# A fused attention and gMLP block on one core: head sums in pairs, and another order of loads and bias at the front

## The chip, the core and the metric

The kernel runs on one core of a Trainium2 chip. The metric is the device time of one execution in microseconds (us); the median of three runs is 208.47 us, from 208.3 to 208.62. A profile of one execution goes with it. Names of engines: PE is TensorE (PEld its weight loads), DVE is VectorE, ACT is ScalarE, POOL is GpSimd, SP is SyncE, which only issues DMAs here. An engine with a q behind its name is that engine's queue of DMA issues.

## The reference

x has 2048 tokens of 512 features, bf16. It is normalized once (xn), and two branches and x itself are summed:

```python
xn = layernorm(x)
# A: 32 heads of 16; each token attends to 8 tokens, 2 apart, up to itself
q, k, v = split(xn @ wqkv)
logits[h, s, w] = sum_d q[h, s, d] * k[h, s - 2 * w, d] / 4     # -1e9 ahead of token 0
a = softmax(logits, axis=w) mixed with v[h, s - 2 * w, :] @ wo
# B: gated MLP with a mix over tokens; F = 1376, halves of 688
z1, z2 = split(gelu(xn @ w_in));  z2 = layernorm(z2)
b = (z1 * (w_sp @ z2 + b_sp[:, None])) @ w_out
out = x + a + b
```

## The kernel before

The 2048 tokens are 16 tiles of 128. The order of instructions on every engine is the order of the program text (a manual schedule): a statement's position decides where it stands in the queue of its engine, and nothing is moved by a planner. Waits come from data and from buffers that are used again.

*Front (lines 91 to 397).* SP issues the loads in the order of lines 166 to 178: tokens of tile 0, of tile 1, the first half of w_z2 (the z2 half of w_in, 2 of 4 k-chunks), tokens of tiles 2 and 3, the second half of w_z2, tokens 4 to 7, q and k weights, tokens 8 to 11, wv, the bias b16, tokens 12 to 15. The x buffers (xqp) are three, so the load of tokens 12 to 15 into the fourth group needs the first buffer back. spin(n) issues n matmuls of a tile of ones into a PSUM tile that nobody reads. DVE takes statistics (ln_stats, L185 and L186) and normalizes (ln_apply, L190). Tiles 0 to 3 are transposed by TensorE (transpose_pe, L212; copied out by ACT for tiles 0 and 1, by DVE for 2 and 3), tiles 4 to 15 by DMA transposes on SP's queue (transpose_dma, L219), in groups of two whose 1/sqrt is worked out by DVE and POOL (ln_newton). z2_part(i, pz, kc) issues the two z2 matmuls (344 columns each) of k-chunk kc of tile i; z2_start does all four chunks, z2_gelu evacuates with gelu, z2_square sums squares on ACT.

*Middle (lines 399 to 480).* q and k chunks (qk_pair L272, qk_chunk L260), z2 tiles, v matmuls (v_pair, L285) and attention logits follow one another on TensorE. For logits, DVE multiplies q with shifted k for two window positions at once, products(hb, p) for block hb of 1024 tokens and pair p (L301, two buffers pr), and TensorE sums over the 16 features of each head: reduce_heads(hb, p), 16 matmuls with a 0/1 selector of 32 columns, placed in the four column strips of the array (tile_position, L310), evacuated by ACT (L312). v_pair works in the same strips, 32 matmuls each. softmax_top subtracts the maximum (DVE), softmax_exp is on ACT, softmax_norm on DVE. z2_stats and z2_norm (L252, 16 DVE instructions) normalize z2.

*Late (lines 492 to 661).* mix(j) multiplies token tile j of w_sp with z2 (32 matmuls, L493) and adds the bias column b_col[:, j] on ACT (L496); z1_tile(j) computes the z1 half (L505, gelu L510); gate_out(j) multiplies on DVE (L515) and transposes by DMA. Between them DVE works off the attention mix (av_ops, L559 to L568). At the end TensorE multiplies with wo and w_out (L636, L647, L622) and DVE adds x.

PSUM: bank_pair gives two-bank tiles in turn from three, ps_aux two one-bank tiles for transposes, pb and head sums. The bias is a row vector of 16 x 128 that pb (L405) transposes into columns.

Of the kernel before, what the change touches and what calls it, by code (L numbers as in the profile page):

```python
# [7 lines left out]
BF16 = mybir.dt.bfloat16  # L8
# [5 lines left out]
P = 128  # L14
S = 2048
D = 512
NT = S // P
C = D // P
# [10 lines left out]
F = 1376  # L29
FH = 688  # L30
# [15 lines left out]
def kernel(  # L46
# [17 lines left out]
    A = nc.scalar  # L64
    G = nc.gpsimd
    PE = nc.tensor
    SP = nc.sync
# [17 lines left out]
    def bank_pair(name, two=False):  # L85
        turn[0] += 1
        pool = ps_b if turn[0] % 3 == 0 and not two else ps_a
        return pool.tile([P, 2, 512], F32, name=name, tag="mm")


    ones = const.tile([P, 256], BF16, name="ones")
    V.memset(ones[:], 1.0)
    idle = bank_pair("idle")

    def spin(n):
        for _ in range(n):
            PE.matmul(idle[:, 0, 0:256], ones[:, 0:P], ones[:], start=True, stop=True)

    spin(17)

    ident = const.tile([P, P], BF16, name="ident")
    G.memset(ident[:], 0.0)
# [11 lines left out]
    G.affine_select(out=mask[:], in_=mask[:], compare_op=ALU.is_ge, fill=NEG,  # L114
                    base=-DIL * (W - 1), pattern=[[DIL, W], [1, HALO]], channel_multiplier=0)
    b_col = const.tile([P, NT], F32, name="b_col")
    b16 = const.tile([NT, P], BF16, name="b16")
    stats = const.tile([P, NT, 6], F32, name="stats")
    mv = const.tile([P, NT, 2], F32, name="mv")
    rstd = const.tile([P, NT], F32, name="rstd")  # L120
# [37 lines left out]
    xq = []  # L158

    def load_x(b):  # L160
        t = xqp.tile([P, 4, D], BF16, name="xq")
        SP.dma_start(t[:], x2[b * 4 * P:(b + 1) * 4 * P, :].rearrange("(i p) d -> p i d", p=P))
        xq.append(t)

    x0 = xqp.tile([P, 4, D], BF16, name="xq")
    SP.dma_start(x0[:, 0, :], x2[0:P, :])
    SP.dma_start(x0[:, 1, :], x2[P:2 * P, :])
    SP.dma_start(w_z2[:, 0:2, :], w_in_r[:, 0:2, FH:F])
    SP.dma_start(x0[:, 2:4, :], x2[2 * P:4 * P, :].rearrange("(i p) d -> p i d", p=P))
    SP.dma_start(w_z2[:, 2:4, :], w_in_r[:, 2:4, FH:F])  # L170
    xq.append(x0)
    load_x(1)
    for s in range(2):
        SP.dma_start(wqk[:, :, s, :], wqkv_r[:, :, s * D:(s + 1) * D])
    load_x(2)
    SP.dma_start(wv[:], wqkv_r[:, :, 2 * D:3 * D])
    SP.dma_start(b16[:], B_b_sp.rearrange("(j p) -> j p", p=P))
    load_x(3)
    V.memset(qk[0][:, 1, :, 0:HALO], 0.0)
    V.memset(vp[0:32, :, 0, 0:HALO], 0.0)  # L180
# [2 lines left out]
    def ln_stats(i):  # L183
        xs = xq[i // 4][:, i % 4, :]
        V.bn_stats(stats[:, i, :], xs)  # L185
        V.bn_aggr(mv[:, i, :], stats[:, i, :])  # L186

    def ln_apply(i):
        xn = xnp.tile([P, D], BF16, name="xn")
        V.tensor_scalar(xn[:], xq[i // 4][:, i % 4, :], mv[:, i, 0:1], rstd[:, i:i + 1], ALU.subtract, ALU.mult)  # L190
        return xn

    def roots(a, b):
        A.activation(rstd[:, a:b], mv[:, a:b, 1], ACT.Sqrt, bias=eps_t[:])
# [14 lines left out]
    def transpose_pe(i, xn):  # L209
        pt = ps_aux.tile([P, C, P], BF16, name="pt", tag="aux")  # L210
        for c in range(C):
            PE.transpose(pt[:, c, :], xn[:, c * P:(c + 1) * P], ident[:])  # L212
        if i < 2:
            A.copy(xnT[:, :, i * P:(i + 1) * P], pt[:])
        else:
            V.tensor_copy(xnT[:, :, i * P:(i + 1) * P], pt[:])

    def transpose_dma(i, xn):
        SP.dma_start_transpose(xnT[:, :, i * P:(i + 1) * P], xn[:])  # L219

    def z2_start(i):
        pz = bank_pair("pzb")
        for kc in range(C):
            z2_part(i, pz, kc)
        return pz

    def z2_part(i, pz, kc):
        for hh in range(2):
            PE.matmul(pz[:, hh, 0:FHALF], xnT[:, kc, i * P:(i + 1) * P],  # L229
                      w_z2[:, kc, hh * FHALF:(hh + 1) * FHALF],  # L230
                      start=(kc == 0), stop=(kc == C - 1))
# [5 lines left out]
    def z2_square(i):  # L237
        A.activation(junk[:], z2[:, i, :], ACT.Square, accum_out=zsq[:, i:i + 1])  # L238

    def z2_tile(i):  # L240
        z2_gelu(i, z2_start(i))
# [13 lines left out]
    def qk_chunk(b, c):  # L255
        tsl = slice(b * 512, (b + 1) * 512)
        pq = bank_pair("pq")
        for s in range(2):
            for kc in range(C):
                PE.matmul(pq[:, s, :], wqk[:, kc, s, c * P:(c + 1) * P], xnT[:, kc, tsl],  # L260
                          start=(kc == 0), stop=(kc == C - 1))
        at = HALO + b % 2 * 512
        A.copy(qk[b // 2][:, :, c, at:at + 512], pq[:])  # L263
# [16 lines left out]
    def v_pair(d2):  # L280
        pv = bank_pair("pv")
        for dd in range(2):
            for kc in range(C):
                for k in range(NG):
                    PE.matmul(pv[32 * k:32 * k + 32, dd, :].rearrange("p (b t) -> p b t", b=NB),  # L285
                              wv_v[:, kc, 2 * d2 + dd, :], xnT_g[:, kc, :, k, :],
                              start=(kc == 0), stop=(kc == C - 1), tile_position=(0, 32 * k))
        A.copy(vp[:, 2 * d2:2 * d2 + 2, :, HALO:HALO + TG],
               pv[:].rearrange("p a (b t) -> p a b t", b=NB))
# [8 lines left out]
    def products(hb, p):  # L298
        pr = prp.tile([P, 2, C, SB], BF16, name="pr")
        off = HALO - DIL * (W - 1 - 2 * p)  # L300
        V.tensor_tensor(pr[:], qk[hb][:, 0, :, HALO:HALO + SB].unsqueeze(1).broadcast_to([P, 2, C, SB]),  # L301
                        shifted(qk[hb][:, 1, :, off:off + SB]), ALU.mult)
        prs[hb, p] = pr

    def reduce_heads(hb, p):
        pr = prs.pop((hb, p))
        pl = ps_aux.tile([P, 2, TG], F32, name="pl", tag="aux")
        for c in range(C):
            for k in range(NG):
                PE.matmul(pl[32 * k:32 * k + 32, :, :], rsel[:, c, :], pr[:, :, c, k * TG:(k + 1) * TG],  # L310
                          start=(c == 0), stop=(c == C - 1), tile_position=(0, 32 * k))
        A.activation(lg[hb][:, 2 * p:2 * p + 2, :], pl[:], ACT.Copy, scale=float(DH) ** -0.5)  # L312

    def softmax_top(hb):
        l = lg[hb]
        if hb == 0:
            V.tensor_tensor(l[0:32, :, 0:HALO], l[0:32, :, 0:HALO], mask[:], ALU.add)
        m4 = lgp.tile([P, 4, TG], BF16, name="m4", bufs=1)
        V.tensor_tensor(m4[:], l[:, 0:4, :], l[:, 4:8, :], ALU.max)
        V.tensor_tensor(m4[:, 0:2, :], m4[:, 0:2, :], m4[:, 2:4, :], ALU.max)  # L320
        V.tensor_tensor(m4[:, 0, :], m4[:, 0, :], m4[:, 1, :], ALU.max)
        V.tensor_tensor(l[:], l[:], m4[:, 0, :].unsqueeze(1).broadcast_to([P, W, TG]), ALU.subtract)
# [24 lines left out]
    def recip(i):  # L347
        V.reciprocal(rstd[:, i:i + 1], rstd[:, i:i + 1])

    ln_stats(0)  # L350
    roots(0, 1)
    ln_stats(1)
    roots(1, 2)
    recip(0)
    transpose_pe(0, ln_apply(0))
    recip(1)
    spin(2)
    transpose_pe(1, ln_apply(1))
    spin(2)
    pz0 = bank_pair("pzb")  # L360
    pz1 = bank_pair("pzb")
    for i, pz in ((0, pz0), (1, pz1)):
        for kc in range(2):
            z2_part(i, pz, kc)
    ln_stats(2)
    roots(2, 3)
    ln_stats(3)
    roots(3, 4)
    for kc in range(2, C):
        z2_part(0, pz0, kc)  # L370
    z2_gelu(0, pz0)
    recip(2)
    xn2 = ln_apply(2)
    recip(3)
    xn3 = ln_apply(3)
    transpose_pe(2, xn2)
    for kc in range(2, C):
        z2_part(1, pz1, kc)
# [8 lines left out]
    for g in groups + (None,):  # L387
        if g:
            for i in range(*g):
                ln_stats(i)  # L390
            ln_newton(*g)
        if prev:
            for i in range(*prev):
                transpose_dma(i, ln_apply(i))
        prev = g


# [3 lines left out]
    z2_square(1)  # L401
    qk_pair(0, 1, 0)
    qk_pair(0, 1, 1)
    pb = ps_aux.tile([P, NT], BF16, name="pb", tag="aux")
    PE.transpose(pb[:], b16[:], ident[0:NT, 0:NT])  # L405
    A.copy(b_col[:], pb[:])
    z2_tile(4)
    z2_square(2)
    z2_tile(5)
# [20 lines left out]
    qk_chunk(2, 1)  # L430
    z2_square(7)
    qk_chunk(2, 2)
    reduce_heads(0, 0)
    products(0, 2)
    v_pair(0)
    qk_chunk(2, 3)
    z2_tile(8)
    qk_chunk(3, 0)
    z2_square(8)
    qk_chunk(3, 1)  # L440
    reduce_heads(0, 1)
    products(0, 3)
    v_pair(1)
    qk_chunk(3, 2)
    z2_tile(9)
    qk_chunk(3, 3)
    z2_square(9)
    z2_tile(10)
    reduce_heads(0, 2)
    products(1, 0)  # L450
    v_pair(2)
    z2_square(10)
    z2_tile(11)
    z2_square(11)
    z2_tile(12)
    reduce_heads(0, 3)
    softmax_top(0)
    products(1, 1)
    v_pair(3)
    z2_square(12)  # L460
    z2_tile(13)
    z2_square(13)
# [1 line left out]
    z2_square(14)  # L464
    z2_tile(15)
    z2_square(15)


    v_pair(4)
    z2_stats()  # L470
    z2_norm()
    v_pair(5)
    reduce_heads(1, 0)
    products(1, 2)
    softmax_exp(0)
    v_pair(6)
# [36 lines left out]
    def gate_out(j):  # L513
        gs, z1 = gate.pop(j)
        V.tensor_tensor(z1[:, 0:FH], gs[:].rearrange("p a b -> p (a b)"), z1[:, 0:FH], ALU.mult)  # L515
        SP.dma_start_transpose(uT[:, :, j * P:(j + 1) * P], z1[:])

    g0 = mix(0)
    reduce_heads(1, 1)
    products(1, 3)  # L520
    z1_tile(0, g0)
    g1 = mix(1)
    reduce_heads(1, 2)
    softmax_norm(0, lgp)
    z1_tile(1, g1)
    gate_out(0)
    reduce_heads(1, 3)
    softmax_top(1)
    gate_out(1)
    z1_tile(2, mix(2))  # L530
    softmax_exp(1)
    att.close()

# [157 lines left out]
```

## Time and profile before

| | us |
|---|---|
| median of 3 runs | 208.47 |
| time of the profiled execution | 208.18 |
| span of its records | 206.5 |
| DVE, ACT, POOL busy | 166.2, 93.6, 16.1 |
| first spin on PE | 1.25 |
| first z2 matmul | 6.61 |
| first DMA transpose issued | 15.03 |
| mix(0) begins | 73.39 |
| last output tile added on DVE | 203.44 |

The span runs from the first to the last recorded instruction; 1.7 us of the execution's time lie around it. The profile gives for each engine its busy time, for each idle time what ended it, and the chain of work that ended last, followed back from the end. Matmuls are pipelined: a group's printed length holds the modelled end of its last matmul, so the distance from one start to the next tells more than a printed length. Starts of groups in the chain lie some 0.1 us behind those in the timeline for the same reason.

### The profile page before, as it was taken

The numbers are of one execution on the slowest core, as the hardware profiler recorded it, in microseconds if no ns is written. First come the engines' busy times: TensorE is split into PE (matmuls) and PEld (weight loads), VectorE is DVE, ScalarE is ACT, GpSimd is POOL, SyncE is SP. The second block draws the span as 40 slices with busy tenths as digits, with TensorE's granted clock in tenths as the row PEclk, the third lists the DMA queues.
The fourth block names the chain that finished last, engine by engine and source line by source line (L and its number), as shares of the span: only waits on it lengthen the run. The fifth ranks groups of instructions, "written<-read, shape, count | busy, mean of one in ns | idle before, by whom it ended". The sixth has DMA issues, their size and how long they took to land.

```text
span 206.5 us, 4016 instructions
## 1 busy us (share of the span) xinstructions
PE 201.7 (98%) x1644; PEld 118.3 (57%) x1644; DVE 166.2 (81%) x192; ACT 93.6 (45%) x145; POOL 16.1 (8%) x82
## 2 busy tenths in 40 slices
PE   7999999999999999999999999999999999999994
PEld 4754544545556665566666666666666664444442
DVE  4899939958369699999999999999999955582353
ACT  3777887675689996328633322123333311000000
POOL 5045630000000000000000000000000000000000
PEclk9999999999999999999999999999999999999999
DMA  6996546978000004623975999999544233036432
GB/s 166 318 344 101 103 101 146 236 136 157 3 0 3 3 0 43 134 51 76 174 156 123 231 179 195 217 190 187 122 141 120 45 79 42 25 97 209 115 104 90
DMA packets 67410, 25.63 MB, mean 124 GB/s; under 512 B 57168, under 2 KB 67264, under 8 KB 67264
## 3 DMA queue, kind: packets, MB, share of 16 engines
q1 hardware_dynamic: 67008, 25.24, 57.6%
q8 instruction: 13, 0.21, 0.4%
q10 hardware_dynamic: 384, 0.13, 0.3%
q14 instruction: 5, 0.04, 0.1%
HBM read 9.79 MB, written 2.10 MB: 58 GB/s over the span
## 4 chain that ended last, share of the span: by engine, by line
PE 91%; DVE 3%; DMA 3%; POOL 1%; issue 1%
PE pg L493 36%; PE pq L260 10%; PE po L647 10%; PE pz L505 9%; PE pzb L229 8%; PE pv L285 7%; PE po L636 6%; PE pl L310 4%; DMA xnT<-xn 2%; DVE stats L185 2%; DMA xq<-in_A_x_dram 1%; PE pt L212 1%; PE po L622 1%; DVE xn L190 1%; DVE mv L186 0%
## 5 line engine op out<-in xcount | busy, mean ns | idle before, releaser
L493 PE MATMUL pg<-z,wspT 128*128 128x344 bf16 x512 | 77.3, 309 | 0.0
L493 PEld LDWEIGHTS <-wspT 128*128 128x128 bf16 x512 | 49.9, 98 | 25.2 <-issue 0.8
L301 DVE TENSOR_TENSOR pr<-qk 128x8192 bf16<-128x8192 bf16 x8 | 35.1, 4425 | 6.5 <-PE pl L310 6.5
L496 ACT ACTIVATE gs<-pg,b_col 128x688 bf16<-128x688 f32 x16 | 13.3, 834 | 54.1 <-PE pg L493 54.1
L559 DVE TENSOR_TENSOR pw<-vp,a_sb 128x4096 bf16<-128x4096 bf16 x16 | 36.1, 2285 | 0.0
L651 DVE TENSOR_TENSOR ot<-po,xr 128x512 bf16<-128x512 f32 x15 | 10.2, 689 | 15.2 <-PE po L647 15.1
L260 PE MATMUL pq<-xnT,wqk 128*128 128x512 bf16 x96 | 21.7, 379 | 0.0
L505 PE MATMUL pz<-w_z,xnT 128*128 128x344 bf16 x128 | 21.3, 309 | 0.0
L229 PE MATMUL pzb<-w_z,xnT 128*128 128x344 bf16 x128 | 20.6, 309 | 0.3 <-DMA xnT<-xn 0.3
L647 PE MATMUL po<-wout,uT 128*128 128x512 bf16 x90 | 19.8, 379 | 0.0
L564 DVE TENSOR_TENSOR pw<-pw 128x4096 bf16<-128x4096 bf16 x8 | 18.3, 2288 | 0.1
L229 PEld LDWEIGHTS <-xnT 128*128 128x128 bf16 x128 | 12.0, 98 | 7.7 <-issue 0.8
L505 PEld LDWEIGHTS <-xnT 128*128 128x128 bf16 x128 | 12.4, 98 | 6.8 <-issue 0.8
L260 PEld LDWEIGHTS <-wqk 128*128 128x128 bf16 x96 | 9.2, 98 | 11.1 <-issue 0.8
L647 PEld LDWEIGHTS <-uT 128*128 128x128 bf16 x90 | 8.7, 98 | 11.0 <-issue 0.8
L285 PE MATMUL pv<-xnT,wv 128*32 128x512 bf16 x256 | 14.9, 380 | 0.0
L263 ACT CAST qk<-pq 128x1024 bf16<-128x1024 f32 x12 | 12.1, 1012 | 5.8 <-PE pq L260 5.8
L510 ACT ACTIVATE z<-pz 128x688 bf16<-128x688 f32 x16 | 11.9, 743 | 5.6 <-PE pz L505 4.8
L238 ACT ACTIVATE junk<-z 128x688 bf16<-128x688 bf16 x16 | 12.4, 778 | 0.1
L636 PE MATMUL po<-wo_r,op 32*128 32x512 bf16 x224 | 12.4, 374 | 0.0
L185 DVE BATCH_NORM_STATS2 stats<-xq 128x6 f32<-128x512 bf16 x16 | 10.8, 674 | 1.9 <-DMA xq<-in_A_x_dram 1.9
L234 ACT ACTIVATE z<-pzb 128x688 bf16<-128x688 f32 x16 | 11.8, 736 | 1.0 <-PE pzb L229 1.0
(79 smaller groups left out, 166.7 us busy)
## 6 DMA issues: line engine op xcount, KB each, us to landing
xr<-in_A_x_dram SPq DMA_DIRECT2D x4, 512.0 KB, 4.1
out_dram<-ot SPq DMA_DIRECT2D x15, 128.0 KB, 1.7
wo_r<-in_A_wo_dram SPq DMA_DIRECT2D x4, 448.0 KB, 5.0
xq<-in_A_x_dram SPq DMA_DIRECT2D x3, 512.0 KB, 8.4
wqk<-in_A_wqkv_dram SPq DMA_DIRECT2D x2, 512.0 KB, 7.5
w_z<-in_B_w_in_dram SPq DMA_DIRECT2D x2, 344.0 KB, 4.3
w_z<-in_B_w_in_dram SPq DMA_DIRECT2D x1, 688.0 KB, 7.2
wout<-in_B_w_out_dram SPq DMA_DIRECT2D x1, 640.0 KB, 4.7
```

The lines of the kernel that those rows point to most:

```text
L185: V.bn_stats(stats[:, i, :], xs)
L229: PE.matmul(pz[:, hh, 0:FHALF], xnT[:, kc, i * P:(i + 1) * P], w_z2[:, kc, hh * FHALF:(hh + 1) * FHALF], start=(kc == 0), stop=(kc == C - 1))
L260: PE.matmul(pq[:, s, :], wqk[:, kc, s, c * P:(c + 1) * P], xnT[:, kc, tsl], start=(kc == 0), stop=(kc == C - 1))
L285: PE.matmul(pv[32 * k:32 * k + 32, dd, :].rearrange("p (b t) -> p b t", b=NB), wv_v[:, kc, 2 * d2 + dd, :], xnT_g[:, kc, :, k, :], start=( ...
L301: V.tensor_tensor(pr[:], qk[hb][:, 0, :, HALO:HALO + SB].unsqueeze(1).broadcast_to([P, 2, C, SB]), shifted(qk[hb][:, 1, :, off:off + SB]), ...
L493: PE.matmul(pg[:, hh, 0:FHALF], wsps[j][:, k, :], z2[:, k, hh * FHALF:(hh + 1) * FHALF], start=(k == 0), stop=(k == NT - 1))
L496: A.activation(gs[:], pg[:, :, 0:FHALF], ACT.Identity, bias=b_col[:, j:j + 1])
L505: PE.matmul(pz[:, hh, 0:FHALF], xnT[:, kc, j * P:(j + 1) * P], w_z1[:, kc, hh * FHALF:(hh + 1) * FHALF], start=(kc == 0), stop=(kc == C - 1))
L559: V.tensor_tensor(pw[:], shifted(vp[:, :, hb, off:off + P]), a_sb[:, 2 * p:2 * p + 2, osl].unsqueeze(2).broadcast_to([P, 2, DH, P]), ALU.mult)
L564: V.tensor_tensor(pws[p - 1][:], pws[p - 1][:], pw[:], ALU.add)
L636: PE.matmul(pos[jj, k][:], op[32 * k:32 * k + 32, d, jj * P:(jj + 1) * P], wo_r[32 * k:32 * k + 32, d, :], start=(d == 0), stop=((jj, k, d ...
L647: PE.matmul(pos[jj, k][:], uT[:, m, i * P:(i + 1) * P], wout[:, m, :], start=False, stop=(m == MCH - 1))
```

## The change

Head sums. Before, each reduce_heads of block 0 stands ahead of one v_pair, and the later three of block 1 between mix and z1_tile calls. Now reduce_heads(0, 0) and (0, 1) stand together ahead of v_pair(0) and v_pair(1); (0, 2) and (0, 3) ahead of v_pair(2) and v_pair(3); (1, 0) and (1, 1) between v_pair(5) and v_pair(6); (1, 2) and (1, 3) between mix(2) and z1_tile(2). products and softmax calls move with them.

Front. w_z2 is loaded in one DMA behind tokens 0 to 3; z2_start(0) does all chunks of tile 0 before tile 1 begins. wv is loaded behind the DMA transposes of tiles 6 and 7. Tokens 12 to 15 are loaded into a part of a_sb, which is otherwise first written by softmax_exp(0). The bias is loaded by ACT's queue as the first statement, transposed between 26 and 9 spins and copied between the first two square roots. A spin has 128 columns in place of 256, and there are 26 + 9 + 4 + 4 of them in place of 17 + 2 + 2.

```diff
+    b16 = const.tile([NT, P], BF16, name="b16")
+    A.dma_start(b16[:], B_b_sp.rearrange("(j p) -> j p", p=P))
-    ones = const.tile([P, 256], BF16, name="ones")
+    ones = const.tile([P, P], BF16, name="ones")
...
-            PE.matmul(idle[:, 0, 0:256], ones[:, 0:P], ones[:], start=True, stop=True)
-    spin(17)
+            PE.matmul(idle[:, 0, 0:P], ones[:], ones[:], start=True, stop=True)
+    spin(26)
...
-        t = xqp.tile([P, 4, D], BF16, name="xq")
+        t = xqp.tile([P, 4, D], BF16, name="xq") if b < 3 else a_sb[:, 0:4, :]
...
     SP.dma_start(x0[:, 1, :], x2[P:2 * P, :])
-    SP.dma_start(w_z2[:, 0:2, :], w_in_r[:, 0:2, FH:F])
     SP.dma_start(x0[:, 2:4, :], x2[2 * P:4 * P, :].rearrange("(i p) d -> p i d", p=P))
-    SP.dma_start(w_z2[:, 2:4, :], w_in_r[:, 2:4, FH:F])
+    SP.dma_start(w_z2[:], w_in_r[:, :, FH:F])
...
     load_x(2)
-    SP.dma_start(wv[:], wqkv_r[:, :, 2 * D:3 * D])
-    SP.dma_start(b16[:], B_b_sp.rearrange("(j p) -> j p", p=P))
     load_x(3)
...
+    pb = ps_aux.tile([P, NT], BF16, name="pb", tag="aux")
+    PE.transpose(pb[:], b16[:], ident[0:NT, 0:NT])
+    spin(9)
     ln_stats(0)
     roots(0, 1)
+    A.copy(b_col[:], pb[:])
     ln_stats(1)
...
-    spin(2)
+    spin(4)
     transpose_pe(1, ln_apply(1))
-    spin(2)
-    pz0 = bank_pair("pzb")
-    pz1 = bank_pair("pzb")
-    for i, pz in ((0, pz0), (1, pz1)):
-        for kc in range(2):
-            z2_part(i, pz, kc)
+    spin(4)
...
-    for kc in range(2, C):
-        z2_part(0, pz0, kc)
+    pz0 = z2_start(0)
     z2_gelu(0, pz0)
...
+    pz1 = bank_pair("pzb")
+    for kc in range(2):
+        z2_part(1, pz1, kc)
     transpose_pe(2, xn2)
...
                 transpose_dma(i, ln_apply(i))
+            if prev[0] == 6:
+                SP.dma_start(wv[:], wqkv_r[:, :, 2 * D:3 * D])
...
-    pb = ps_aux.tile([P, NT], BF16, name="pb", tag="aux")
-    PE.transpose(pb[:], b16[:], ident[0:NT, 0:NT])
-    A.copy(b_col[:], pb[:])
...
     qk_chunk(2, 2)
-    reduce_heads(0, 0)
-    products(0, 2)
-    v_pair(0)
     qk_chunk(2, 3)
...
     qk_chunk(3, 1)
+    reduce_heads(0, 0)
     reduce_heads(0, 1)
+    products(0, 2)
     products(0, 3)
+    v_pair(0)
     v_pair(1)
...
     z2_tile(10)
+    z2_square(10)
+    z2_tile(11)
     reduce_heads(0, 2)
+    reduce_heads(0, 3)
     products(1, 0)
     v_pair(2)
-    z2_square(10)
-    z2_tile(11)
+    products(1, 1)
+    softmax_top(0)
     z2_square(11)
+    v_pair(3)
     z2_tile(12)
-    reduce_heads(0, 3)
-    softmax_top(0)
-    products(1, 1)
-    v_pair(3)
...
     reduce_heads(1, 0)
+    reduce_heads(1, 1)
     products(1, 2)
...
     g0 = mix(0)
-    reduce_heads(1, 1)
     products(1, 3)
     z1_tile(0, g0)
     g1 = mix(1)
-    reduce_heads(1, 2)
     softmax_norm(0, lgp)
     z1_tile(1, g1)
     gate_out(0)
+    g2 = mix(2)
+    reduce_heads(1, 2)
     reduce_heads(1, 3)
     softmax_top(1)
     gate_out(1)
-    z1_tile(2, mix(2))
+    z1_tile(2, g2)
```

More of the change, by code (lines that the diff above doesn't have):

```diff
@@ L116 @@
     b_col = const.tile([P, NT], F32, name="b_col")
-    b16 = const.tile([NT, P], BF16, name="b16")
     stats = const.tile([P, NT, 6], F32, name="stats")
@@ L160, in load_x @@
     def load_x(b):
-        t = xqp.tile([P, 4, D], BF16, name="xq")
-        SP.dma_start(t[:], x2[b * 4 * P:(b + 1) * 4 * P, :].rearrange("(i p) d -> p i d", p=P))
+        t = xqp.tile([P, 4, D], BF16, name="xq") if b < 3 else a_sb[:, 0:4, :]
+        SP.dma_start(t[:] if b < 3 else t, x2[b * 4 * P:(b + 1) * 4 * P, :].rearrange("(i p) d -> p i d", p=P))
         xq.append(t)
```

## The prediction

> **What bounds the kernel now.** I read the busy shares first, then the chain of work that ended last, then the timeline of TensorE over the first 23 us, then the DMA landings, then VectorE's timeline. The shares of the page:
>
> ```profile
> PE 201.7 (98%) x1644; PEld 118.3 (57%) x1644; DVE 166.2 (81%) x192; ACT 93.6 (45%) x145; POOL 16.1 (8%) x82
> ```
>
> TensorE is at work for all but a few us, and from 20.56 us to 203.4 us the chain consists of PE pieces alone. So there are only two ways to shorten the span: less time inside the PE pieces, or an earlier moment at which the gapless stretch begins. Pieces of the chain (start, length, what):
>
> ```profile
> 36.32 0.98 PE pl L310 x16
> 37.30 1.73 PE pv L285 x32
> 39.03 1.83 PE pq L260 x8
> ...
> 51.18 1.73 PE pq L260 x8
> ...
> 69.14 0.86 PE pl L310 x16
> ```
>
> Head sums (pl) and v matmuls (pv) use the array in column strips (128*32 in the page's groups), everything around them uses 128*128. A head sum entered from 128*128 work takes 0.98, one between v matmuls (69.14) takes 0.86: entering costs 0.12. The q/k chunk that follows strips takes 1.83, one that follows 128*128 work takes 1.73: leaving costs 0.10. Between pl and pv nothing is paid. **One strip stage costs 0.22 us of overhead.**
>
> TensorE at the front, twice (start, duration, instruction, in brackets the idle time and its releaser):
>
> ```profile
> 6.39 0.38 PE L97 MATMUL idle<-ones 128*128 128x256 bf16 x2
> 6.61 1.96 PE L229 MATMUL pzb<-w_z,xnT 128*128 128x344 bf16 x12
> 8.41 0.39 PE L212 MATMUL pt<-ident,xn 128*128 128x128 bf16 x4
> ```
>
> ```profile
> 18.46 0.38 PE L272 MATMUL pq<-xnT,wqk 128*128 128x512 bf16 x1
> 18.77 0.18 PE L405 MATMUL pb<-ident,b 16*128 16x16 bf16 x1
> 18.91 1.34 PE L229 MATMUL pzb<-w_z,xnT 128*128 128x344 bf16 x8
> 20.56 0.61 PE L229 MATMUL pzb<-w_z,xnT 128*128 128x344 bf16 x3 [0.31 <-DMA xnT<-xn]
> ```
>
> Twelve matmuls in 8.41 - 6.61 = 1.80 us is 0.15 each, so the ninth, the first that needs the second half of w_z2, starts at 7.81. That half was issued at 2.70 and took 5.1 us: it landed at 7.8, with no slack. DMA landings (KB, us from issue to landing; the 688 KB one is w_z1, later in the kernel):
>
> ```profile
> w_z<-in_B_w_in_dram SPq DMA_DIRECT2D x1, 344.0 KB, 5.1
> ```
>
> ```profile
> w_z<-in_B_w_in_dram SPq DMA_DIRECT2D x1, 688.0 KB, 7.2
> ...
> xq<-in_A_x_dram SPq DMA_DIRECT2D x2, 128.0 KB, 2.1
> ...
> uT<-op ACTq DMA_DIRECT2D x8, 16.0 KB, 3.9
> ...
> b<-in_B_b_sp_dram SPq DMA_DIRECT2D x1, 4.0 KB, 7.3
> ```
>
> **Part 1, head sums in pairs.** Strip stages before: (00 v0), (01 v1), (02 v2), (03 v3), (v4 v5 10 v6 v7), (11), (12), (13), eight, where 02 is the head sum of block 0, pair 2. In the order of instructions of the new kernel: (00 01 v0 v1), (02 03 v2 v3), (v4 v5 10 11 v6 v7), (12 13), four. Matmuls are the same in number. 4 x 0.22 = **-0.88 us** on the path.
>
> What the new order makes later is VectorE, since products have two buffers and a product waits for the head sum two before it. Laid out on the old clock, with the chain's lengths: q/k chunks to 42.67, head sum 00 to 43.65 instead of 37.3. The third product runs 43.75 to 48.2 (before, it followed at once: 13.09 for three from 31.15), the fourth to 52.6; head sum 03 starts at 56.0, so 3.4 us of slack. Head sum 02 ends at 56.0 (before 55.05), the products of block 1 run to 64.95, softmax_top (2.97, from 61.48 to 64.45 before) to 67.9. z2_stats started at 68.78 before, so it is not later. zrstd hangs on ScalarE's queue there (squares, v copy, table load at 69.55), which I lay out 0.2 earlier at most. mix(0) starts 0.86 later for head sum 11 and 0.44 earlier for two stages: 73.88.
>
> ```profile
> 71.47 6.00 DVE L252 TENSOR_SCALAR z<-z,zmean,zrstd 128x688 bf16<-128x688 bf16 x16
> ```
>
> The sixteenth tile is ready at 77.47, and mix(0) wants it at 73.46 + 15/16 x 4.67 = 77.84: 0.37 of cover before, about 0.8 after. If z2_norm came later than that, mix(0) would lose the difference one to one. softmax_top(1) now waits for head sum 13 (ends 92.17, plus 0.6 of evacuation): 92.9 instead of 92.18. VectorE runs about 0.8 late from there while TensorE is 0.9 early. This is covered:
>
> ```profile
> 171.01 0.52 DVE L515 TENSOR_TENSOR z<-gs,z 128x688 bf16<-128x688 bf16 x1 [2.90 <-ACT z L510]
> ```
>
> 2.90 idle here, 4.01 before 177.74, and op is done at 182.28 where TensorE asks for it at 186.77. Cost 0; without that cover 0.8.
>
> **Part 2, bias transposed at the beginning.** Out of the path go pb and its surroundings: the last q/k matmul before it is issued at 18.46 and lasts 0.216 (6.91/32), so z2_tile(4) could start at 18.68 instead of 18.91: **-0.23**. In its new place pb stands between 26 and 9 spins. Spins before: 17 of 256 columns, 1.25 to about 4.9, some 0.213 each; 35 of half that width are 3.73 us, with pb about 0.1 it ends near 5.1, before xn of token tile 0 (5.18). This needs the bias by 1.2 + 26 x 0.107 = 4.0. Behind SP's queue it took 7.3; alone on ACT's queue at 0.8 it stands nearest to the first 128 KB of x, 2.1 (2.9), the other ACT-queue row gives 3.9 (4.7). At 4.7 tile 0 starts 0.6 late, which the wait in part 3 hides; at 8.1 it would cost 1.7. I take 2.9, cost 0. Its issue and the table load (1.28) on ScalarE end before mv is there at 3.9; b_col's copy (0.18) fits between the two square roots (3.92+0.29 and 4.71). The removed copy on ScalarE at 19.79 is off the path.
>
> **Part 3, w_z2 in one load.** All of z2_start(0) now waits for all 688 KB. It is issued at 2.19, with the same 1200 KB ahead and in it as the second half had (landed 7.8, issued 2.70). Low end: the stretch from 4 to 5 us moved 331 GB/s, and next to nothing moved before 2 us, so 1200 KB could be over by 5.7 and told by about 6.1, before w_z2 is wanted (6.61): shift 0. High end: w_z1's 7.2 us as one load, 9.39: shift 2.8. I take the row with the same bytes at the same place, moved by the issue it saves (0.51): **7.3**, a shift of 0.7 with the start latency. Everything behind moves with it: transposes of tiles 2 and 3, VectorE's copies of them, statistics of tile 4 onward and the DMA transposes. **+0.7 us.** The 4 + 4 spins of 128 take what 2 + 2 of 256 took.
>
> The Trainium skill, "DMA: Bandwidth & Descriptors", section "Anatomy of one DMA — SWDGE (gpsimd) path", fits a load as 2.0 us plus bytes over 436 GB/s (on another queue type than SP's). By that, as an estimate, 688 KB land 3.6 us after issue at 5.8, nothing waits, and the sum would be 0.7 better; the trace's 5.1 and 7.2 speak against it.
>
> **Part 4, wv behind the transposes, x tiles 12 to 15 into a_sb.** 512 KB less lie ahead of the first DMA transposes, and the bias too. Tile 4's took 3.8 and tile 5's 4.1 (16.41 to 20.52) against a median of 2.5. z2_tile(5) could start at 18.91 + 1.17 = 20.08 and started at 20.56: **-0.48**. What is late next: with the shift s, tile 5 is issued at 16.4+s and lands 18.9+s, wanted 19.85+s; tile 7 issued 19.2+s lands 21.7+s, wanted 22.2+s. If landing stays near 3.5 to 4, 0.45 comes back; this end I keep for the range. wv itself is wanted at about 44 and lands near 25; SP's queue gets it before tile 8's transpose, whose group is wanted at 31 and then lands by 28. a_sb is written first by softmax_exp(0) at 73.9: no wait.
>
> **The sum.** -0.88 - 0.23 - 0.48 + 0.7 = -0.9 us. On the profiled execution, 208.18 (span 206.5), 207.3. The median of the runs shown, 208.47, lies 0.3 above it: **207.6** against the median. Less than 0.2%, 0.42 us, can't be told from no change.
>
> **Rivals.**
> - *The front eats the pairs* (0.22): w_z2 lands at 7.8 to 8.6, or strip stages do not cost what I read. Landing at 8.2 gives a shift of 1.6 and a sum of 0: 208.5. If pairs gave nothing, the front alone is -0.0: 208.5 as well. For it: the ninth matmul had no slack before and the first eight have now lost their early half. Against: issue is 0.5 earlier.
> - *w_z2 late, slower* (0.18): one load of 688 KB behaves as w_z1's did, 7.2, landing 9.39. Shift 2.8: sum +1.2, 209.7. It decides from a landing at 8.6 (+0.42). For it: the only whole load of this size in the trace. Against: w_z1 shared the engines with transposes of w_sp.
> - *Nothing waits* (part of the forecast's case): landing before 6.6, sum -1.6, 206.9.
>
> **Chances.** Forecast, landing from 6.6 to 7.8, -1.6 to -0.4: 0.60. Same 0.22, slower 0.18. Range 206.8 to 208.8: it holds the first two cases and the beginning of the third.
>
> Idle matmuls of 256 columns start 0.213 apart until about 6.2 us and 0.108 apart behind it, and TensorE then stays at the short distance. The Trainium skill, "TensorE: Matmul & The Clock Gate", section "What's actually happening", says that about 3.4 us without work bring the half rate back. By it a wait of 0.7 or of 2.8 costs only itself; were a wait enough to bring it back, the twelve first matmuls alone would take another 1.8. No row here shows it either way.
>
> **What would show it.** Right: pl pieces of 0.98 only at the head of four stages, each stage's follower 0.10 longer; a PE wait on w_z2 of about 0.7 near 6.6 us; no wait before z2_tile(5); no pb at 18.8; mix(0) gapless. Wrong: a DMA wait of over 1.5 us there, a VectorE releaser ahead of mix(0) or of the last PE stage, a late bias that holds the first transposes.

## The result and the profile after

The changed kernel takes 206.69 us (median of 4 runs, 206.6 to 206.94); the kernel before, beside it, 208.38 (4 runs, 208.25 to 208.62). The ratio is 0.992, interval 0.9902 to 0.9937: 1.7 us less, where 0.9 was predicted, and 0.1 below the low end of the range. The profiled execution took 206.6, its span 204.9, against 208.18 and 206.5: 1.6 us less, which the lines below account for.

The page of the changed kernel, its span and its busy shares:

```profile
span 204.9 us, 4056 instructions
...
PE 200.3 (98%) x1660; PEld 120.7 (59%) x1666; DVE 166.1 (81%) x192; ACT 93.5 (46%) x145; POOL 16.1 (8%) x82
```

TensorE is busy 1.4 us less, and its share is 98% as before: no idle time has come in the place of what went.

The chain of work that ended last, of the changed kernel (start, length, what): the strip stages, then mix(0).

```profile
42.11 1.84 PE pl L310 x32
43.95 3.45 PE pv L285 x64
...
50.41 1.73 PE pq L260 x8
...
54.47 1.84 PE pl L310 x32
56.31 3.45 PE pv L285 x64
...
68.15 1.73 PE pl L310 x32
69.87 3.45 PE pv L285 x64
73.33 4.77 PE pg L492 x32
...
89.77 1.84 PE pl L310 x32
91.61 1.27 PE pz L504 x8
```

Two head sums of 32 matmuls entered from other work take 1.84, that is 2 x 0.86 + 0.12; the pair that stands between v matmuls (68.15) takes 1.73. Leaving costs 0.10 (the z1 tile of 1.27 beside its usual 1.17). There are four stages instead of eight, each at the price that was read from before. From 12.38 to the last output add the chain holds PE pieces and five pieces of "issue" of 0.05 to 0.16 us, each beside a group whose records are one matmul short (47 of 48, 41 of 42 in the po groups). mix(0) begins without a wait.

TensorE at the front of the changed kernel (timeline: start, duration, instruction):

```profile
4.00 0.19 PE L351 MATMUL pb<-ident,b 16*128 16x16 bf16 x1
...
6.46 0.39 PE L100 MATMUL idle<-ones 128*128 128x128 bf16 x4
6.83 1.91 PE L229 MATMUL pzb<-w_z,xnT 128*128 128x344 bf16 x12
8.58 0.39 PE L212 MATMUL pt<-ident,xn 128*128 128x128 bf16 x4
...
18.85 3.66 PE L229 MATMUL pzb<-w_z,xnT 128*128 128x344 bf16 x24
22.35 1.89 PE L260 MATMUL pq<-xnT,wqk 128*128 128x512 bf16 x7
```

The load of w_z2 in the changed kernel, by its line (shortest, median and longest issue in ns, when, and below it the time to landing):

```profile
L172 SPq DMA_DIRECT2D w_z<-in_B_w_in_dram x1: 469/469/469, 2.2 to 2.2; - x1
...
DMA to landing us min/median/max: 4.6/4.6/4.6
```

The one load of 688 KB lands at 2.2 + 4.6 = 6.8, not at 7.3, and the first z2 matmul starts at 6.83 instead of 6.61; 0.07 of this lateness is there already at the last idle matmuls (6.46 instead of 6.39). The twelve first matmuls take 1.75 instead of 1.80: before, the fifth, the first of tile 1, came some 0.05 late. So the front is late by 0.17. Without pb, z2_tile(4) is nevertheless 0.06 earlier than before, and the three z2 tiles behind it take 22.35 - 18.85 = 3.50 instead of 4.00, since the wait ahead of z2_tile(5) is gone. The q/k chunk behind them, predicted to start where it did, starts at 22.35 instead of 22.91.

Where the 1.6 us of the two profiles lie (from mix(0) on by the chain, whose starts lie 0.07 behind the timeline's, so that each column adds up to 0.07 less than its span):

| stretch | before | after | difference |
|---|---|---|---|
| start to the q/k chunk of tokens 4 to 7 | 22.91 | 22.35 | -0.56 |
| from there to mix(0) | 50.48 | 50.91 | +0.43 (head sum 11 moved here +0.86, two stages fewer -0.43) |
| mix(0) to the first po | 96.69 | 95.38 | -1.31 (head sum 11 gone -0.86, two stages fewer -0.45) |
| first po to the last output add | 33.29 | 33.30 | 0.0 |
| last add to the end of the span | 3.06 | 2.89 | -0.17 |

VectorE has the idle time that was counted on. In the changed kernel's timeline of VectorE, z2_norm begins ahead of mix(0) (73.26 there), and softmax_top(1) waits for its head sums:

```profile
70.52 6.00 DVE L252 TENSOR_SCALAR z<-z,zmean,zrstd 128x688 bf16<-128x688 bf16 x16
...
92.29 0.69 DVE L319 TENSOR_TENSOR m<-lg 128x1024 bf16<-128x1024 bf16 x1 [0.98 <-ACT lg L312]
```

### The profile page after: what moved, and what is told of

The parts are those of the page before. It is cut to its first block, busy times and chain, and to the rows that moved or that the text cites. A ratio compares the mean times of both kernels' runs of the same rounds, so it can differ in the third digit from the quotient of the medians.

```text
span 204.9 us, 4056 instructions
## 1 busy us (share of the span) xinstructions
PE 200.3 (98%) x1660; PEld 120.7 (59%) x1666; DVE 166.1 (81%) x192; ACT 93.5 (46%) x145; POOL 16.1 (8%) x82
## 4 chain that ended last, share of the span: by engine, by line
PE 96%; DVE 1%; DMA 1%; issue 0%
PE pg L492 36%; PE pq L260 10%; PE po L646 9%; PE pzb L229 9%; PE pz L504 9%; PE pv L285 7%; PE po L635 6%; PE pl L310 4%; PE pq L272 3%; DMA xq<-in_A_x_dram 1%; PE po L621 1%; PE pt L212 1%; DVE stats L185 1%; PE idle L100 0%; DVE xn L190 0%
## 5 line engine op out<-in xcount | busy, mean ns | idle before, releaser
L650 DVE TENSOR_TENSOR ot<-po,xr 128x512 bf16<-128x512 f32 x15 | 10.2, 689 | 15.2 <-PE po L646 14.9
L229 PE MATMUL pzb<-w_z,xnT 128*128 128x344 bf16 x128 | 20.1, 309 | 0.0
L646 PE MATMUL po<-wout,uT 128*128 128x512 bf16 x88 | 19.3, 379 | 0.3 <-issue 0.3
L285 PEld LDWEIGHTS <-wv 128*32 128x32 bf16 x256 | 9.4, 139 | 4.6 <-issue 0.3
```

The lines of the kernel that those rows point to most:

```text
L646: PE.matmul(pos[jj, k][:], uT[:, m, i * P:(i + 1) * P], wout[:, m, :], start=False, stop=(m == MCH - 1))
```

## The experiments

Each run is compared with the kernel before on the same chip (208.11 to 208.18 as median there); "the kernel after" has 206.69 against 208.38. My theory: head sums in pairs give 0.9, and the front 0.7, through a load that lands earlier than I had put it and a wait that disappears. The rivals: the front gives nothing or all of it; wv's new place, not the load, took the wait away; one load in itself is slower than halves, and something else pays for it.

**Each half of the change alone.** e1_pairs_only is the kernel before with the new order of reduce_heads, products, softmax_top and v_pair, and nothing of the front. e2_front_only is the kernel after with those in the old order (the first lines of its edit):

```diff
     qk_chunk(2, 2)
+    reduce_heads(0, 0)
+    products(0, 2)
+    v_pair(0)
     qk_chunk(2, 3)
...
-    reduce_heads(0, 0)
     reduce_heads(0, 1)
```

> The kernel before with the head sums in pairs alone. Theory: four strip stages fewer at 0.22 us each, 0.88 us less, about 207.5 against 208.4, and the front as before (second half of w_z2 just in time, a DMA wait ahead of z2_tile(5)). Rival: the pairs bring more than that (all of the 1.7) because other waits in the middle go with them; or nothing, and the whole gain is the front's: 208.4.

> The changed kernel with the head sums in the old order, so the front alone. Theory: the first q/k chunk of tokens 4 to 7 starts 0.56 us earlier, the rest of the chain is unchanged: 0.6 to 0.8 less, 207.6 to 207.8. w_z2 lands near 6.8 us again, since the loads are the same. Rival: the landing of 6.8 was one lucky execution; then it lands nearer to 7.3 in this profile and the time is 208.2 or more.

Measured: e1 207.35 (206.94 to 208.01), ratio 0.9959 (0.9943 to 0.9975), -0.83. e2 207.51 (207.37 to 208.21), 0.9973 (0.9962 to 0.9983), -0.67. Together -1.50 of -1.69: within their intervals they add up, and neither is nothing. The pairs are what was worked out (0.88); it is the front, predicted at 0.0, that gave the rest. In e2 w_z2 again landed at 6.8.

The profiles say it more sharply than the medians. From the q/k chunk of tokens 4 to 7 to the last output add it is 180.53 or 180.54 us in each profile with eight strip stages (before, e2, e10) and 179.65 or 179.66 in each with four (the kernel after, e1, e3 to e9, e11), so four stages are worth 0.88. What else differs between these profiles lies ahead of that chunk or behind the last add, and the part ahead varies for one and the same front too: the chunk starts at 22.91 in the profile of before and at 23.48 in that of e1, whose front is that of before.

**The load in halves, two ways.** e3_halves goes back to the halves around tokens 2 and 3 with the z2 order of before; e4_halves_behind only splits the load where it is:

```diff
-    SP.dma_start(w_z2[:], w_in_r[:, :, FH:F])
+    SP.dma_start(w_z2[:, 0:2, :], w_in_r[:, 0:2, FH:F])
+    SP.dma_start(w_z2[:, 2:4, :], w_in_r[:, 2:4, FH:F])
```

> The changed kernel, but w_z2 in two halves around tokens 2 and 3 and the z2 matmuls of tiles 0 and 1 interleaved, as before. Theory: the single load costs at most the 0.2 us for which it is awaited, so with halves the first z2 matmul starts at 6.6 to 6.7 and the time is the same within 0.2, perhaps 0.1 to 0.2 less: 206.5 to 206.7. Rival: the one load behind the tokens makes the whole landing earlier (6.8 against 7.8) and the halves bring a wait back: tiles 2 and 3 or the second half late by 0.2 to 0.5, 206.9 to 207.2.

> The changed kernel with w_z2 in two loads one behind the other, both behind tokens 2 and 3; matmuls as in the changed kernel. Tells why it landed at 6.8 and not at 7.3. Theory order: what counts is that all bytes of x go first and the DMA engines stay supplied; the second half lands within 0.2 of 6.8, time within 0.2 of 206.7. Rival issue: the landing follows the issue, which is 0.5 later for the second half, so it lands at 7.3 and the time is 207.2.

Measured: e3 206.51 (206.26 to 206.93), 0.9919 (0.9907 to 0.9932); e4 206.85 (206.47 to 207.88), 0.9936 (0.9916 to 0.9955). By the measured time neither can be told from the kernel after. In the profiles, though, the second half landed at 8.3 in e3 and at 7.8 in e4, later than either side of e4's expectation (6.8 or 7.3). TensorE in e3, which starts z2 earlier than any and then waits:

```profile
6.21 1.34 PE L230 MATMUL pzb<-w_z,xnT 128*128 128x344 bf16 x8
8.39 0.74 PE L230 MATMUL pzb<-w_z,xnT 128*128 128x344 bf16 x4 [0.83 <-DMA w_z<-in_B_w_in_dram]
```

What the engines move meanwhile, in windows of 1 us (the last two columns are the share of the DMA engines' time and GB/s), first e1 (halves), then the kernel after:

```profile
5.00:6.00 1.00, 0.87 (x7) 0.71 (x7) 0.87 (x4) 0.16 (x1) 0.00 (x0) 1.00 0.89 277
6.00:7.00 1.00, 1.00 (x11) 0.85 (x9) 0.97 (x3) 0.85 (x2) 0.00 (x0) 1.00 0.68 164
7.00:8.00 1.00, 0.97 (x7) 0.41 (x5) 0.93 (x5) 0.85 (x4) 0.00 (x0) 1.00 0.93 297
```

```profile
5.00:6.00 1.00, 0.93 (x10) 0.67 (x8) 0.96 (x4) 0.13 (x2) 0.00 (x0) 1.00 1.08 378
6.00:7.00 1.00, 1.00 (x14) 0.84 (x12) 0.96 (x3) 0.90 (x2) 0.00 (x0) 1.00 1.05 365
7.00:8.00 1.00, 1.00 (x9) 0.66 (x8) 0.86 (x4) 0.98 (x4) 0.00 (x0) 1.00 1.09 378
```

In the profiles with halves the rate falls at 6 to 7 us (164 GB/s in e1, 194 in e3, 218 before, 297 in e4); in the seven with one load behind tokens 2 and 3 on SP's queue it does not (365 after, 372 in e2, 351 in e6, 340 to 367 in the others). The bytes ahead are the same. The second half landed at 7.8, 8.9, 8.3 and 7.8 in the four profiles with halves, the whole load between 6.6 and 7.0 in the seven.

The dip is not a matter of halves alone: one load behind tokens 4 to 7, an experiment further down, has it too (281 GB/s at 6 to 7 us in e5; 204 at 5 to 6 and 175 at 6 to 7 in e9). In all six profiles with a dip a load of w_z2, whole or half, is the fifth on SP's queue, issued near 2.7; in the seven without, all of w_z2 is the fourth, issued near 2.2. No run tells form and place apart.

Nor are these profiles all typical. Those of e1, e3 and e4 were among the slower executions of their kernels (207.87 of 206.94 to 208.01; the slowest of five; the second slowest of six). In e3's, the earlier first z2 does not pay for the wait: its q/k chunk starts at 22.74 instead of 22.35, and it took 206.93 instead of 206.6. So e3's other executions, 206.26 to 206.84, lost less at the front; where their halves landed is not known. What halves cost in the median is not shown to be more than nothing.

**One load alone, in the kernel before.** e10_one_load_only is the kernel before with one load and the z2 order of tile 0 first; wv, the x buffers, the bias and the head sums stay as they were:

```diff
-    SP.dma_start(w_z2[:, 0:2, :], w_in_r[:, 0:2, FH:F])
     SP.dma_start(x0[:, 2:4, :], x2[2 * P:4 * P, :].rearrange("(i p) d -> p i d", p=P))
-    SP.dma_start(w_z2[:, 2:4, :], w_in_r[:, 2:4, FH:F])
+    SP.dma_start(w_z2[:], w_in_r[:, :, FH:F])
```

> The kernel before with one part of the front alone: w_z2 in one load behind tokens 0 to 3, and all of tile 0's z2 matmuls ahead of tile 1's. Theory: w_z2 lands near 6.9 in place of 7.8 to 8.9, the first z2 matmul waits 0.2, but z2_tile(5) still waits for its transpose behind the late load of tokens 12 to 15: 0 to 0.4 less, 207.8 to 208.2. Rival: the one load is the whole front, 0.6 to 0.8 less, 207.4 to 207.6.

Measured: 207.89 (207.74 to 208.18, and one of 210.94 at a mean granted clock of 0.992), 0.9987 (0.9976 to 0.9998). w_z2 landed at 6.6. The stream behind it was earlier as well: tokens 8 to 11 at 12.9 instead of 13.7, wv 14.3 instead of 15.3, tokens 12 to 15 at 15.8 instead of 18.0. TensorE of e10, to be held against the 18.91, 20.56 and 22.91 of before:

```profile
18.89 3.72 PE L228 MATMUL pzb<-w_z,xnT 128*128 128x344 bf16 x24
22.45 7.07 PE L259 MATMUL pq<-xnT,wqk 128*128 128x512 bf16 x32
```

The wait ahead of z2_tile(5) is gone, with wv where it was. Between these two profiles the one load, which I had put at +0.7, took away most of the wait that I had credited to wv. The median gains 0.2, the profile 0.4 (207.79): the time is in the theory's range, but the wait that the theory kept did not come, and the rival's 0.6 to 0.8 did not either.

The wait itself stands in one profile only. e1 has the front of before, and its three tiles run without it, though its w_z2 was 1.1 later and its first DMA transpose was issued at 16.11 instead of 15.03:

```profile
19.96 3.67 PE L229 MATMUL pzb<-w_z,xnT 128*128 128x344 bf16 x24
23.48 6.85 PE L260 MATMUL pq<-xnT,wqk 128*128 128x512 bf16 x30
```

The transposes of tiles 4 and 5 took 3.8 and 4.1 us in the profile of before, 2.8 and 3.3 in e10, 2.5 both in e1, where tokens 12 to 15 landed about as late as before (18.0).

**wv and the x buffer by themselves.** e6_wv_early puts wv back ahead of tokens 12 to 15; e11_x3_buffer puts these tokens back into the first x buffer:

```diff
+    SP.dma_start(wv[:], wqkv_r[:, :, 2 * D:3 * D])
     load_x(3)
```

```diff
-        t = xqp.tile([P, 4, D], BF16, name="xq") if b < 3 else a_sb[:, 0:4, :]
+        t = xqp.tile([P, 4, D], BF16, name="xq")
```

> The changed kernel with wv loaded ahead of tokens 12 to 15 again, which still go into a_sb without a wait for a buffer. Theory wv: its 512 KB ahead of the transposes make tile 5 late by up to 0.5 again: 207.0 to 207.2. Rival buffer: in the kernel before, the transposes were late because the load of tokens 12 to 15 waited for its buffer and was still running at 18 us; without that wait everything is over by about 15.3, tile 4's transpose, issued at 15.2, takes some 2.6 and the time is within 0.2 of 206.7.

> The changed kernel with tokens 12 to 15 in the first x buffer again, so that their load waits until tokens 0 to 3 are normalized; wv stays behind the transposes. Theory: the load is issued near 8.7 and has nothing but tokens 8 to 11 ahead of it, so it is over by about 15.5, tile 5's transpose is not late, time within 0.2 of 206.7: it took wv and the buffer together to make it late. Rival: the wait for the buffer alone brings 0.3 to 0.5 back, 207.0 to 207.2.

Measured: e6 206.86 (206.6 to 207.04), 0.9933 (0.9919 to 0.9947); e11 206.73 (206.4 to 207.12), 0.9929 (0.9912 to 0.9946). Neither costs anything that can be told from the kernel after. No wait came back ahead of z2_tile(5): the three tiles take 3.50 in both, though in e6 tokens 12 to 15 landed at 17.2 instead of 14.2. Neither move by itself was needed for that gain. Together they may be enough without the one load: e3 and e4, with halves and both moves, have 3.50 as well.

**The bias.** e7_bias_mid puts pb and its copy back ahead of z2_tile(4), with the bias still loaded early:

```diff
-    pb = ps_aux.tile([P, NT], BF16, name="pb", tag="aux")
-    PE.transpose(pb[:], b16[:], ident[0:NT, 0:NT])
     spin(9)
...
+    pb = ps_aux.tile([P, NT], BF16, name="pb", tag="aux")
+    PE.transpose(pb[:], b16[:], ident[0:NT, 0:NT])
+    A.copy(b_col[:], pb[:])
     z2_tile(4)
```

> The changed kernel with the bias transposed and copied where it was before, between the q/k matmuls of tokens 0 to 3 and z2_tile(4); its load stays at the beginning. Theory: 0.1 to 0.25 more, 206.8 to 206.95, and z2_tile(4) starts that much later behind the last q/k matmul. Rival: it was hidden behind the transposes' landing and costs nothing: 206.7.

Measured: 206.91 (206.74 to 206.98), 0.9936 (0.9923 to 0.995). From the first q/k matmul to z2_tile(4) it is 7.11 instead of 6.91: +0.20, where 0.23 was predicted. The medians differ by 0.2 too, but their intervals overlap.

**What a late w_z2 costs.** e5_w_z2_later puts the load behind tokens 4 to 7, so that it must come late; e9_w_z2_later_warm does the same and covers the wait with idle matmuls:

```diff
-    SP.dma_start(w_z2[:], w_in_r[:, :, FH:F])
     xq.append(x0)
     load_x(1)
+    SP.dma_start(w_z2[:], w_in_r[:, :, FH:F])
```

```diff
     transpose_pe(1, ln_apply(1))
-    spin(4)
+    spin(60)
```

> The changed kernel with w_z2's load behind tokens 4 to 7 as well, 512 KB more ahead of it. Theory: the first z2 matmul starts when w_z2 lands, at about 8.3 us instead of 6.8, and everything behind it moves by the same 1.5: 208.1 to 208.4. Rival: something later absorbs part of a late front (the DMA transposes, VectorE), and less than half of the 1.5 reaches the end: below 207.5.

> As the run with w_z2 behind tokens 4 to 7 (median 210.95, first z2 matmul at 9.77 after 3.0 us idle, the twelve first matmuls 3.36 us in place of 1.75), with 60 spins in place of the last 4, so that TensorE is at work until about 9.75. Theory clock: the idle 3.0 us brought the half rate back; with spins the twelve take 1.75 again and the time is about 1.6 less, 209.3. Rival: the twelve were slow for another reason (w_z2 or xnT still being written), they take over 3 us again and the time stays at 210.5 to 211.

Measured: e5 210.95 (208.59 to 212.22), 1.0112 (1.0078 to 1.0147); e9 209.6 (209.08 to 210.07), 1.0066 (1.0042 to 1.0091). w_z2 landed at 9.7 in e5 and at 10.2 in e9, not near the 8.3 that both sides of e5's expectation took. TensorE in e5:

```profile
6.40 0.39 PE L100 MATMUL idle<-ones 128*128 128x128 bf16 x4
9.77 3.52 PE L229 MATMUL pzb<-w_z,xnT 128*128 128x344 bf16 x12 [2.99 <-DMA w_z<-in_B_w_in_dram]
13.13 0.39 PE L212 MATMUL pt<-ident,xn 128*128 128x128 bf16 x4
```

The windows of e5, whose first of the last three columns is the granted clock:

```profile
9.00:10.00 1.00, 0.23 (x1) 0.10 (x1) 0.00 (x0) 0.00 (x0) 0.00 (x0) 0.84 1.02 335
10.00:11.00 1.00, 1.00 (x5) 0.58 (x4) 0.00 (x0) 0.00 (x0) 0.00 (x0) 0.50 1.08 381
```

And TensorE in e9:

```profile
6.13 3.51 PE L100 MATMUL idle<-ones 128*128 128x128 bf16 x60
10.23 1.91 PE L229 MATMUL pzb<-w_z,xnT 128*128 128x344 bf16 x12 [0.58 <-DMA w_z<-in_B_w_in_dram]
11.97 0.39 PE L212 MATMUL pt<-ident,xn 128*128 128x128 bf16 x4
```

In e5 TensorE idles for 2.99 (3.20 from the start of its last idle matmul), the granted clock is 0.50 from 9.7 to 13.1, and the twelve matmuls take 3.36, 0.28 each instead of 0.146: 1.61 lost beside the 2.94 of lateness. The q/k chunk starts at 26.90, 4.55 later than after, and the profiled execution (211.16) is 4.56 longer: a loss at the front arrives at the end one to one. In e9 the twelve matmuls, though they start 0.46 later, take 1.74, and the profiled execution (209.99) is 1.17 shorter; 0.46 + 1.17 = 1.63 is the price of the half rate, measured a second way.

The half rate did not come back in every execution of e5. Four have a mean granted clock of 0.992 and took 210.72 to 211.32 us; 3.4 us at 0.50 in some 209 give such a mean. One with 0.983 took 212.22. One with 1.000 took 208.59, a loss of 1.9; how long TensorE idled there is not recorded.

**The load on the other queue.** e8_w_z2_act issues w_z2 from ACT's queue behind the bias:

```diff
     x0 = xqp.tile([P, 4, D], BF16, name="xq")
+    A.dma_start(w_z2[:], w_in_r[:, :, FH:F])
     SP.dma_start(x0[:, 0, :], x2[0:P, :])
...
-    SP.dma_start(w_z2[:], w_in_r[:, :, FH:F])
```

> The changed kernel with w_z2's one load issued by ACT's queue behind the bias (about 1.25 us) and not by SP behind tokens 2 and 3 (2.19). Theory: the first z2 matmul waits for w_z2 by up to 0.3, so a landing ahead of 6.5 brings 0.1 to 0.3: 206.4 to 206.6. Rival: w_z2 shares the DMA engines with the tokens, tiles 0 to 3 land later by 0.3 to 0.8, and the time is 206.9 to 207.4.

Measured: 207.15 (nine executions 206.89 to 207.29, three 208.51 to 208.60), 0.9963 (0.9944 to 0.9982): worse than the kernel after, in the rival's range. The weights landed at 6.75, no earlier than from SP's queue, while tokens of tile 1 came at 4.4 instead of 3.6 and tiles 2 and 3 at 7.0 instead of 4.9. The tokens now share the engines: at 5 to 6 us ACT's queue moved 0.10 MB and SP's 0.23. In the profile (one of the three) the first transposes start at 5.89, 0.63 after the last spin, and the twelve matmuls take 2.90:

```profile
7.58 3.06 PE L229 MATMUL pzb<-w_z,xnT 128*128 128x344 bf16 x12
10.48 0.39 PE L212 MATMUL pt<-ident,xn 128*128 128x128 bf16 x4
```

Until 9.87 they start 0.29 apart, from 10.04 on 0.146. The windows of this stretch give a granted clock of 1.00 throughout, as they do for the slow idle matmuls from 1.1 to 4 us in every profile, so the slow pace of a front is read from the starts and not from that column.

**One stage fewer.** e12_three_stages joins the second and third strip stage: z2 tiles 12 to 15 go ahead of head sums (0, 2) and (0, 3), v_pair(2) to v_pair(6) behind them, and softmax_top(0) behind z2_norm:

```diff
     z2_tile(10)
+    z2_tile(11)
     z2_square(10)
-    z2_tile(11)
+    z2_tile(12)
...
+    z2_tile(15)
     reduce_heads(0, 2)
     reduce_heads(0, 3)
...
+    v_pair(6)
     reduce_heads(1, 0)
     reduce_heads(1, 1)
+    softmax_top(0)
     products(1, 2)
-    softmax_exp(0)
-    v_pair(6)
```

> A version built on the strip rule: the second and third strip stage joined (z2 tiles 12 to 15 go ahead of them), v matmuls standing between the head sums of block 0 and of block 1 while VectorE makes the products; z2_norm goes ahead of softmax_top(0), softmax_exp(0) behind mix(0). Theory: one stage less, 0.22 less than the changed kernel, 206.4 to 206.5, if head sum (1, 1) does not wait for its product and z2_norm starts by 71.4. Rival: VectorE's later products make head sum (1, 1) or mix(0) wait by over 0.3, 206.9 or more.

Measured: 206.45 (four executions 206.28 to 206.47, two 207.28 and 207.29), 0.9929 (0.9906 to 0.9952). The stretch from the q/k chunk to mix(0) is 50.64 in its profile instead of 50.91: -0.27, one stage (0.22) and a little. Its median is the lowest of all, but its interval doesn't tell it from the kernel after; why two executions took 0.8 more is not known.

## Why the prediction was right in direction and wrong in size

1. *Strip stages, -0.88: right.* Four stages of 0.12 in and 0.10 out are gone: -0.43 ahead of mix(0) and -0.45 behind it in the profiles, -0.83 (0.5 to 1.2) in the medians of e1, and -0.27 for a fifth stage in the profile of e12.
2. *VectorE's later products cost 0: right.* z2_norm began at 70.52, 0.95 earlier than before, so mix(0) didn't wait; of the 2.90 idle ahead of the last gate 1.4 is left. The wait of softmax_top(1) for head sum 13 (0.98) was foreseen and is covered.
3. *Bias, -0.23: right.* 0.20 in e7. It landed at 2.9 as taken, pb ran at 4.00, and b_col's copy stood at 4.23 between the two roots.
4. *"I take the row with the same bytes at the same place, moved by the issue it saves (0.51): 7.3 ... +0.7 us": this step failed.* The load landed at 6.8, and the front was late by 0.17: the term was 0.5 too high, and this is most of the 0.7 by which the sum missed the profile. I took the row of a half, fifth on the queue, for the whole load in fourth place. In the four profiles with halves the rate falls at 6 to 7 us and the second half lands at 7.8 to 8.9; in the seven with one load behind tokens 2 and 3 the rate holds and all of it has landed by 7.0. My low end, "over by 5.7 and told by about 6.1", was too low; the high end of 9.39, from w_z1, was not near. The rival "w_z2 late" is false here, but its price was too low too: in e5 a landing 2.9 later cost 4.55.
5. *The wait ahead of z2_tile(5), -0.48: right in size (-0.50), but its reason is not shown, and the size is luck in part.* I gave it to wv's 512 KB out of the way. e6 and e11 undo each move alone and keep the gain; e10 has neither and has most of it, so wv's place was not needed. The size is that of one profile: e1, with the loads of before, has no such wait, on a later front. I had added 0.7 of lateness and 0.48 of relief as if they were independent; in e10 the one load brings the relief and hardly any lateness (first z2 matmul at 6.67 instead of 6.61).
6. *"By it a wait of 0.7 or of 2.8 costs only itself": not so close to the long one.* No wait of the kernel after comes near 2.8. e5 and e9 show that 2.99 without work bring back a granted clock of 0.50 and cost 1.6 more; 2.8 itself was not measured. The Trainium skill, "TensorE: Matmul & The Clock Gate", section "What's actually happening", names about 3.4 us without work for the return of the half rate; the trace has it after 2.99, and the measurement decides.

By its own terms the sum is then -0.88 - 0.23 - 0.50 + 0.17 = -1.44 on the profiled execution; the 0.16 that is missing to the 1.6 of the spans lies behind the last output add, in a part that the change doesn't touch; that stretch takes 2.8 to 3.1 in the other profiles, so it varies by as much anyway. The remaining 0.2 of the 0.9 is not in the sum: the profile of before lay 0.3 below its median and I kept that distance, while the profile after lies 0.1 below its own. "Nothing waits" (-1.6, 206.9) is the case whose time came, without its condition: w_z2 did not land before 6.6.

Left open: why the rate falls at 5 to 7 us in the profiles with halves and in those with one load behind tokens 4 to 7, which landed at 9.7 and 10.2 when its bytes, at the rate of the kernel after, would have been there near 8.3; why the first two DMA transposes of before were slow; and how the front's gain in the medians (0.67 in e2) divides beyond the 0.2 of e10 and the 0.2 of the bias.

## What to carry to other kernels

Where TensorE is the whole chain, count how often the array changes between column strips and full width, price one change from two neighbouring pieces of the chain, and group the work of one kind: the forecast from that (0.88) was met in the profiles, and to 0.05 in the medians. A load's landing at the start belongs to its form and its place in the queue: here a half's time moved by an issue was no estimate of the whole (7.3 against 6.6 to 7.0). The loads behind it moved with it in e10 (tokens 8 to 11 by 0.8), so such a term must not be summed beside waits that the same stream decides. And one profile of a front is one sample: that of before varied by 0.57 between two. Where a load may come some 3 us late, idle matmuls up to 0.6 us before it lands kept the clock here (e9).

## What the runs showed of the hardware that was not expected

- 2.99 us without work on TensorE were followed by a granted clock of 0.50 for 3.4 us (e5), 1.6 us of loss on twelve matmuls of 344 columns; five of e5's six executions have a mean granted clock under 1. With idle matmuls up to 0.58 ahead there was no loss (e9).
- The same first 1200 KB had landed at 7.8 to 8.9 us with w_z2 in halves (four profiles) and at 6.6 to 7.0 in one load (seven). The rate dips to 164 to 297 GB/s at 6 to 7 us with halves, and to 175 and 281 with one load behind tokens 4 to 7; behind tokens 2 and 3 one load kept 340 to 372.
- 688 KB from ACT's queue were there at 6.75, no earlier than from SP's queue at 6.8, and delayed SP's token loads by 0.8 and 2.1 us (e8).
- The moment from which TensorE kept the short distance of matmuls varied between profiles with the same matmuls up to there: the first four transposes took 0.40 from 5.12 us in e11, and 0.61 from 5.25 in e5; in e8 the short distance came only at 10.0.
